# Small value products woven with strips of the neighbouring unit, and layer 0's transposes in half-row tiles: four layers of local attention and gated MLP

## The chip, the cores and the metric

The kernel runs on one NeuronCore of a Trainium2 chip, in one launch. The metric is device time in microseconds (us); lower is better. A profile is taken of one execution with the hardware profiler; its span reaches from the first to the last instruction. TensorE is PE in the profile (its weight loads are PEld), VectorE is DVE, ScalarE is ACT, GpSimd is POOL, SyncE is SP.

## The reference

One sequence of S = 2048 tokens with D = 448 features in bf16 goes through four layers. Layers 0 and 2 are attention with 16 heads of 28 over eight keys, each two positions apart; layers 1 and 3 are a gated product with F = 1792. Both attention layers share weights, and so do both gated ones.

```
def _A_ref(x, wqkv, wo):
    qkv = (x @ wqkv).reshape(B, S, 3, H, Dh).transpose(2, 0, 3, 1, 4)
    q, k, v = qkv[0], qkv[1], qkv[2]
    idx = arange(S)[:, None] - (arange(8) * 2)[None, :]
    logits = einsum("bhsd,bhswd->bhsw", q, k[:, :, idx]) * Dh ** -0.5
    attn = softmax(where(idx >= 0, logits, -1e9))
    o = einsum("bhsw,bhswd->bhsd", attn, v[:, :, idx])
    return o.transpose(0, 2, 1, 3).reshape(B, S, D) @ wo

def _B_ref(x, w_gate, w_up, w_down):
    return ((x @ w_gate) * (x @ w_up)) @ w_down

x = x + _A_ref(layernorm(x), wqkv, wo)
x = x + _B_ref(layernorm(x), w_gate, w_up, w_down)
x = x + _A_ref(layernorm(x), wqkv, wo)
x = x + _B_ref(layernorm(x), w_gate, w_up, w_down)
```

## The kernel before

Everything stays on the chip between layers. Even and odd positions are stored apart, so that the eight keys of a token are neighbours. Tokens are 16 blocks of 128; the chunks that a layer works on are 256 or 512 tokens. A job is one chunk of one layer: `SEQ` names them, A for attention and B for the gated layers ("A00" is layer 0, chunk 0). Jobs of different layers overlap.

A job of an attention layer has these units, in a function each:

- `ln_chunk`: VectorE makes the statistics of each block (`bn`, L630; `mv`, L632), ScalarE the reciprocal deviation (L633, L635), VectorE the normalized block `xn_sb` (L651). It is transposed into `xnTa` or `xnTb`: for layer 0's five chunks (`PE_T`) by TensorE, four 128x128 products a block into one PSUM bank (L660) and a copy by VectorE or ScalarE (L666); for the others by a transposing DMA that SP issues (L654).
- `qk_chunk` and `v_group`: queries, keys and values, from products with 64 rows in two halves of the array (L698, `twin`), copied out of PSUM (L750, L842). The last four heads' values go through DRAM (`PW` copies L759, transposing DMA L770).
- `attn_front`: a score burst, 64 products of 28 rows in tiles of 32x64 (L862), for one group of up to 120 query positions of two blocks; ScalarE's exponential (L869), VectorE's mask (L879).
- `attn_back`: a value burst, 64 products in tiles of 64x32 with 64 columns each (L896; 32 products with 72 columns in a layer's first group), copies into a slot of `O_sb` (L910, L914), and `norm`: a shuffle by VectorE (L924), logarithm and exponential by ScalarE (L925, L926), and VectorE's multiply into `oT` (L937).
- `y_blocks`: output projection (L714, `twin_blocks`) and the addition to `x_sb` (L954).

`b_chunk` is a gated job: for each of 14 slices of F, seven steps of two products with 64 rows, gate in the upper half of the array's rows and up in the lower (L983); ScalarE copies the gate to `g_sb` (L989), VectorE multiplies it with up into `hT` (L992); then products with `WD` for two blocks at a time (L714) and the addition (L954). The last two blocks of the last job end in whole 128x128 tiles, one of 448 columns and two of 224 (L1004, L1008), then output.

A **step** below is what two 64-row products do side by side on the two halves of the array, into two PSUM banks. A **unit** is one `sc.add("pe", ...)` with its steps.

No order is written by hand. Every operation is an `Op` with an estimate, dependencies, a priority (job position plus the tables `PR` and `JP`) and a shape of tiles (`mode`): "R64" (`MAIN`) for 64x128, "R32" for score bursts, "C32" for value bursts, "F" for whole tiles. `Sched.schedule` runs through modelled time and takes for each free engine the ready operation of best priority that finds its PSUM banks; on TensorE it holds units of another shape back (`HOLD_A`, `HOLD_BA`, `HOLD_BB`), since a change of shape has a modelled cost (`SWITCH`). `emit` writes each engine's list in that order, with semaphore waits ahead of each operation. So all estimates and tables shape the order on all five engines, SP's DMAs included.

The head: 48 warm-up products (L565) while inputs load, then the first blocks' transposes.

Of the kernel before, what the change touches and what calls it, by code (L numbers as in the profile page):

```python
# [9 lines left out]
S = 2048  # L10
D = 448
H = 16
DH = 28
F = 1792
# [13 lines left out]
MAIN = "R64"  # L28
PE_T = ("00", "01", "02", "03", "04")
HEAD_LN = 5  # L30
HEAD_P = (-53.71, -30.23, -20.33, -12.94, -19.33)
# [4 lines left out]
S_EST = 270.0  # L36
# [6 lines left out]
VT = 4  # L43
# [8 lines left out]
PR = {'AV': 8.84, 'rstd': -5.66, 'bn': 0.73, 'N': -2.82, 'Gps': -1.08, 'Tps': 16.85, 'H': 18.16, 'S': 10.61, 'VT': 19.61, 'Ex': 16.77, 'G': -2.93, 'xn': -6.19, 'QK': -6.56, 'Ddps': -26.52, 'V': 22.93, 'x': -0.84, 'lnv': -15.5, 'Oc': -6.51, 'Oa': -6.47, 'R': -19.3, 'VVps': 1.22, 'Yps': -25.3, 'PW': 58.69, 'T': -9.57, 'mv': 2.02, 'Rs': -2.57, 'Rl': 21.52, 'QKps': 4.71, 'E': -7.15, 'wqk': -9.31, 'wqp': -11.53}  # L52
JP = {'A20': -3.02, 'B32': 16.28, 'B34': 16.21, 'A22': 20.13, 'B13': 2.73, 'A21': 6.27, 'B12': -2.81, 'A02': -0.21, 'A03': 4.03, 'B30': 4.3, 'B31': 8.23, 'B10': 21.86, 'B11': -14.15, 'A23': 29.86, 'A04': -0.79, 'B33': 153.62, 'A01': -5.33, 'B14': 4.53, 'A00': -24.6}
# [15 lines left out]
A_CAP = 4  # L69
B_CAP = 8  # L70
# [42 lines left out]
class Op:  # L113
    __slots__ = ("engs", "ins", "est", "deps", "mode", "prio", "acquire", "release", "idx", "eng",
                 "dma", "lat", "after", "start", "end", "seen", "selfd", "tmin")
# [14 lines left out]
class Sched:  # L130
# [6 lines left out]
    SWITCH = 92.0  # L137
    FETCH = 4.17
    CREDIT = 36.0
    HICCUP = 210.0  # L140

    def __init__(self):
        self.ops = []
        self.ready = {}
        self.rng = random.Random(SEED)

    def add(self, engs, ins, est, deps=(), prio=0.0, mode=None, acquire=None, release=(), dma=None, lat=0.0, after=None, selfd=(), tmin=None):
        if isinstance(engs, str):
            engs = (engs,)
        if not isinstance(est, dict):  # L150
            est = {e: float(est) for e in engs}
        op = Op(engs=engs, ins=ins, est=est, deps=[d for d in deps if d is not None], mode=mode, prio=prio,
                acquire=acquire, release=release, idx=len(self.ops), dma=dma, lat=lat, after=after, selfd=set(selfd), tmin=tmin)
# [63 lines left out]

    def schedule(self):
# [6 lines left out]
        credit, clast = self.CREDIT, 0.0  # L225
# [6 lines left out]
        for op in self.ops:  # L232
# [9 lines left out]
            if not srcs:  # L242
                for e in op.engs:
                    pend[e].append(op)
        left = len(self.ops)
        now = 0.0
        while left:
            moved = False
            b_ready = any(o.acquire is not None and o.acquire.kind == 1 for o in pend["pe"])
            for e in self.ENGS:  # L250
# [4 lines left out]
                for op in pend[e]:  # L255
                    r = self.ready_at(op, e)
                    if r <= now + 1e-6:
                        cands.append((op.prio, op.idx, op))
# [40 lines left out]
                if best is None:  # L299
                    continue  # L300
                op = best
                op.eng = e
                for x in op.engs:
                    pend[x].remove(op)
                if op.acquire is not None:
                    op.acquire.b = self.pick_banks(op.acquire, now)
                    for b in op.acquire.b:
                        self.holder[b] = op.acquire
                        if self.last_rel[b] is not None:
                            op.deps.append(self.last_rel[b])  # L310
                if op.tmin is not None and e == "sp":
                    gate = [o for o in order["pe"] if o.end + self.PE_LAT <= now and isinstance(o.ins[-1][1], tuple) and o.ins[-1][1] in self.ready]
                    op.deps.append(gate[-1].ins[-1][1])
                est = op.est[e]
                if e == "pe":
                    if mode is not None and op.mode != mode:
                        est += self.SWITCH
                    mode = op.mode
                    n = 2 * len(op.ins)
                    credit = min(self.CREDIT, credit + (now - clast) / self.FETCH)  # L320
                    if n > 40:
                        est = max(est, (n - credit) * self.FETCH + (self.HICCUP if n > credit + 40 else 0.0))
                    credit = max(0.0, credit + est / self.FETCH - n)
                    clast = now + est
                op.start, op.end = now, now + est
                free[e] = op.end
                order[e].append(op)
                for bk, i in op.release:
                    b = bk.b[i]
                    assert self.holder[b] is bk  # L330
                    self.holder[b] = None
                    self.free_at[b] = op.end + self.TAIL[op.eng]
                    key = ("rel", op.idx, b)
                    self.ready[key] = (op, len(op.ins) - 1)
                    self.last_rel[b] = key
                left -= 1
                moved = True
                for u in users.get(op.idx, ()):
                    ndep[u.idx] -= 1
                    if ndep[u.idx] == 0:  # L340
                        for x in u.engs:
                            pend[x].append(u)
# [3 lines left out]
            for e in self.ENGS:  # L346
# [4 lines left out]
                else:  # L351
                    c = [self.ready_at(op, e) for op in pend[e]]
# [9 lines left out]
    def emit(self, nc, block, sems):  # L362
# [10 lines left out]
        for e in self.ENGS:  # L373
            for op in self.order[e]:
# [5 lines left out]
                for n in range(len(op.ins)):  # L380
# [42 lines left out]
def pe_cols(n):  # L423
    return n / 2.4 + 2.6
# [710 lines left out]
```

## Time and profile before

| | |
|---|---|
| runs | 392.64, 393.89, 394.48 us; median 393.89 |
| profiled execution, span | 391.9 us, 2.0 below the median run |
| granted TensorE clock | 1.000 |
| instructions | 13910 |
| products on TensorE | 6142 |
| TensorE idle in gaps, by what ended them | "issue" 0.9, a DMA 0.9, VectorE 0.6 + 0.5, start 1.1 us |
| DMA | 22.47 MB, mean 57 GB/s |

The page gives busy time by engine, the chain of work that ended last (each step followed back to what released it), and the costliest groups of instructions: line, engine, operation, output<-inputs, partitions x elements, count, then busy time, mean of one in ns, and the engine's idle time before them with what ended it. "64\*128" on a product is the tile, rows x columns. "issue" marks idle time in which the profile shows nothing to wait for. A timeline row has start, length, engine, line and count of neighbouring instructions of one kind.

### The profile page before, as it was taken

The page shows a single profiled execution, that of the slowest core. Times are in us where ns is not written, and L with a number is a line of the kernel's source. Part 1 is how long each engine was busy: PE and PEld are TensorE (multiplying, and loading weights), DVE is VectorE, ACT ScalarE, POOL GpSimd, SP SyncE. Part 2 cuts the span into 40 slices and gives each one's busy share as a digit, 9 for nine tenths or more (in the row PEclk, how much of TensorE's full clock was granted, in tenths as well). Part 3 has the DMA queues.
Part 4 walks back from the last instruction along what each step waited for, and adds up shares of the span by engine and source line. Part 5 has one row for each costly group of instructions (what it writes and reads, how often), then busy time and mean ns, then how long its engine had stood idle before and what let it go on. Part 6 is the DMA issues. An engine that isn't in the chain of part 4 may idle for free.

```text
span 391.9 us, 13910 instructions
## 1 busy us (share of the span) xinstructions
PE 384.9 (98%) x6142; PEld 213.8 (55%) x6142; DVE 271.2 (69%) x596; ACT 207.3 (53%) x398; POOL 7.6 (2%) x36
## 2 busy tenths in 40 slices
PE   8999999999999999999999999999999999999997
PEld 6655657545444544554546867444454544444674
DVE  6989899669967765684788645258942689477252
ACT  4888876478523745467651523268315782263230
POOL 6010000000000000000000000000000000000000
DMA  8990161501220401320121141010050102403101
GB/s 275 295 306 19 24 93 28 106 13 30 48 49 15 80 15 35 64 28 15 17 49 21 36 95 29 25 20 11 12 128 7 26 7 47 95 4 16 34 27 47
DMA packets 54703, 22.47 MB, mean 57 GB/s; under 512 B 44836, under 2 KB 54644, under 8 KB 54644
## 3 DMA queue, kind: packets, MB, share of 16 engines
q1 hardware_dynamic: 53284, 19.47, 23.7%
q10 hardware_dynamic: 1360, 2.12, 1.8%
q8 instruction: 48, 0.79, 0.8%
q14 instruction: 11, 0.09, 0.1%
HBM read 8.54 MB, written 2.71 MB: 29 GB/s over the span
## 4 chain that ended last, share of the span: by engine, by line
PE 90%; DVE 4%; DMA 2%; ACT 2%; issue 1%; SPq 0%; DVEq 0%
PE ps L983 41%; PE ps L714 25%; PE ps L698 16%; PE ps L896 3%; PE ps L862 3%; PE ps L1004 1%; DMA xnTb<-xn_sb 1%; DMA x_sb<-in_A_x_dram 1%; PE ps L660 1%; DVE xn_sb L651 1%; DVE st L630 1%; DVE x_sb L954 1%; ACT R_sb L925 1%; ACT R_sb L926 1%; DVE E_sb L879 0%
## 5 line engine op out<-in xcount | busy, mean ns | idle before, releaser
L983 PE MATMUL ps<-xnTb,WGU 64*128 64x512 bf16 (+1 forms) x1960 | 180.5, 333 | 0.9 <-DMA xnTb<-xn_sb 0.9
L983 PEld LDWEIGHTS ps<-xnTb,WGU 64*128 64x128 bf16 x1960 | 93.5, 94 | 73.8 <-ACT g_sb L989 1.5
L989 ACT ACTIVATE g_sb<-ps 128x512 bf16<-128x512 f32 (+1 forms) x140 | 71.4, 511 | 95.0 <-PE ps L983 94.3
L992 DVE TENSOR_TENSOR hT<-g_sb,ps 128x512 bf16<-128x512 bf16 (+1 forms) x140 | 79.3, 574 | 55.1 <-ACT g_sb L989 46.1
L714 PE MATMUL ps<-WD,hT 64*128 64x448 bf16 x840 | 84.0, 349 | 0.1
L714 PEld LDWEIGHTS ps<-WD,hT 64*128 64x128 bf16 x840 | 40.2, 94 | 37.0 <-DVE hT L992 0.8
L698 PE MATMUL ps<-xnTa,WQK 64*128 64x512 bf16 (+1 forms) x504 | 53.5, 353 | 0.3
L954 DVE TENSOR_TENSOR x_sb<-x_sb,ps 128x448 bf16<-128x448 bf16 x62 | 36.2, 614 | 24.9 <-PE ps L714 24.8
L630 DVE BATCH_NORM_STATS2 st<-x_sb 128x6 f32<-128x448 bf16 x64 | 37.5, 615 | 2.7 <-DMA x_sb<-in_A_x_dram 2.7
L869 ACT ACTIVATE E_sb<-ps 128x1024 bf16<-128x1024 f32 (+1 forms) x36 | 33.5, 980 | 9.6 <-PE ps L862 9.3
L750 ACT ACTIVATE qk<-ps 128x1024 bf16<-128x1024 f32 (+1 forms) x30 | 27.1, 921 | 19.3 <-PE ps L698 19.0
L651 DVE TENSOR_SCALAR xn_sb<-x_sb,mv,rstd 128x512 bf16<-128x512 bf16 (+1 forms) x64 | 33.7, 569 | 4.7 <-ACT rstd L635 4.5
L698 PEld LDWEIGHTS ps<-xnTa,WQK 64*128 64x128 bf16 x504 | 23.5, 94 | 24.0 <-ACT xnTa L666 0.8
L879 DVE TENSOR_TENSOR E_sb<-E_sb,MK 128x1024 bf16<-128x1024 bf16 (+2 forms) x40 | 23.9, 613 | 8.8 <-ACT E_sb L869 8.5
L714 PE MATMUL ps<-wo_g,oT 64*128 64x448 bf16 x256 | 29.1, 349 | 0.0
L633 ACT ACTIVATE lnv<-mv,eps_sb 128x2 f32<-128x2 f32 (+1 forms) x33 | 9.5, 293 | 30.4 <-DVE mv L632 30.2
L937 DVE TENSOR_TENSOR oT<-O_sb,R_sb 128x480 bf16<-128x480 f32 (+3 forms) x36 | 22.1, 627 | 3.4 <-ACT R_sb L926 3.1
L925 ACT ACTIVATE R_sb<-R_sb 128x480 f32<-128x480 f32 (+1 forms) x34 | 20.1, 600 | 5.6 <-DVE R_sb L924 5.6
L924 DVE STREAM_SHUFFLE R_sb<-O_sb 128x480 f32<-128x480 f32 (+1 forms) x34 | 22.7, 696 | 0.0
L698 PE MATMUL ps<-WV,xnTa 64*128 64x336 bf16 (+3 forms) x252 | 22.2, 304 | 0.2
L926 ACT ACTIVATE R_sb<-R_sb 128x480 f32<-128x480 f32 (+1 forms) x34 | 20.1, 602 | 0.4
L714 PEld LDWEIGHTS ps<-wo_g,oT 64*128 64x128 bf16 x256 | 12.3, 94 | 11.6 <-DVE oT L937 0.4
(47 smaller groups left out, 170.7 us busy)
## 6 DMA issues: line engine op xcount, KB each, us to landing
out_dram<-x_sb SPq DMA_DIRECT2D x15, 112.0 KB, 1.7
WD<-in_B_w_down_dram SPq DMA_DIRECT2D x2, 784.0 KB, 11.5
WGU<-in_B_w_up_dram SPq DMA_DIRECT2D x2, 784.0 KB, 17.6
WGU<-in_B_w_gate_dram ACTq DMA_DIRECT2D x2, 784.0 KB, 13.3
x_sb<-in_A_x_dram SPq DMA_DIRECT2D x3, 448.0 KB, 6.4
vt<-qk SPq DMA_DIRECT2D x42, 16.0 KB
xnTb<-xn_sb SPq DMA_TRANSPOSE x32, 3.0
x_sb<-in_A_x_dram SPq DMA_DIRECT2D x2, 224.0 KB, 4.2
```

The source lines that it names most:

```text
L630: sc.add("dve", one(lambda E, B=B: E.bn_stats(st6[:, B, :], x_sb[:, B, :]), ("bn", li, B)), 525.0, deps=[("x", li - 1, B)] + ([("xn", li - ...
L651: sc.add("dve", one(lambda E, B=B, dst=dst, src=src: E.tensor_scalar(dst, src, mv[:, B, 0:1], rstd[:, B:B + 1], ALU.subtract, ALU.mult), ( ...
L698: parts[0 if s < 3 else 1][1].append((lambda E, w=w, c=c, lo=lo, st=st, sp_=sp_: E.matmul(u["out"](w), u["lhs"](w, c, lo, lo + 64), u["rhs ...
L714: ins.append((lambda E, w=w, c=c, lo=lo, st=st, sp_=sp_: E.matmul(outs(w), lhs(w, c, lo), rhs(w, c, lo), start=st, stop=sp_), keys[w] if s ...
L750: return E.activation(dst, src, ACT.Copy) if hasattr(E, "activation") else E.tensor_copy(dst, src)
L869: return E.activation(E_sb[:, slot, 2 * hp:2 * hp + 2, 0:w], ps[:, b0:b0 + 2, 0:w], ACT.Exp, scale=SCALE)
L925: sc.add("act", one(lambda E: E.activation(R_sb[:, rs, 0:w], R_sb[:, rs, 0:w], ACT.Ln), ("Rl", li, qb)), act_est(w, False), deps=[("Rs", l ...
L926: sc.add("act", one(lambda E: E.activation(R_sb[:, rs, 0:w], R_sb[:, rs, 0:w], ACT.Exp, scale=-1.0), ("R", li, qb)), act_est(w, False), de ...
L954: sc.add("dve", one(lambda E: E.tensor_tensor(x_sb[:, B, :], x_sb[:, B, :], ps[:, bk[w], 0:D], ALU.add), ("x", li, B)), dve_est(D), deps=[ ...
L983: ins.append((lambda E, u=u, k=k, w=w: E.matmul(u["out"](w), WGU[64 * w:64 * w + 64, k, 128 * u["fc"]:128 * u["fc"] + 128], X[64 * w:64 * ...
L989: sc.add("act", one(lambda E, gs=gs, bk=bk: E.activation(g_sb[:, gs, 0:nt], ps[:, bk[0], 0:nt], ACT.Copy), ("G", li, j, fc)), act_est(nt), ...
L992: sc.add("dve", one(lambda E, gs=gs, bk=bk, fc=fc: E.tensor_tensor(hT[:, fc, hs, 0:nt], g_sb[:, gs, 0:nt], ps[:, bk[1], 0:nt], ALU.mult), ...
```

## The change

*Strips.* `crossed`, `twin`, `twin_blocks` and `b_chunk` now hand over their units as steps, and `pair` makes two forms of each: the two products as before, and eight strips of 64x32, four for each half, with the same moving data and columns. When the scheduler places a value burst (`BURST`), it looks for a ready unit in 64x128 tiles, takes it as host, and lays its first steps as strips into the burst: two steps for 64 products (`WEAVE`, `MAXALT`), after 21 and 42 of them, one for 32. The host's remaining steps follow at once in whole products. All waits of burst and host stand ahead of the burst.

*Transposes and warm-up.* A block of layer 0 is transposed by eight products of 64 rows and 64 columns into two banks in place of four of 128x128 into one; the copy reads both banks. The 48 warm-up products become 96 of 64 rows. Their shape is `MAIN`.

*Value bursts* wait for the last reader of the `O_sb` slots that their copies write, which the copies alone waited for.

*The model and its tables.* TensorE's time in the scheduler now has a queue and instruction lines (`run_pe`), other estimates (`S_EST`, `AV_EST`, `SWITCH`), other caps on banks, a limit on how far gate units run ahead (`after`), and `PR`, `JP` and `HEAD_P` are all new. The order on every engine is new.

```diff
+BURST = "C32"
+WEAVE = 2
+MAXALT = 2
...
-S_EST = 270.0
+S_EST = 288.0
+AV_EST = 288.0
...
-A_CAP = 4
-B_CAP = 8
+A_CAP = 6
+B_CAP = 6
...
+                    if op.mode == BURST and WEAVE:
+                        host = next((m for m in okay if m is not op and m.mode == MAIN and len(m.alt) and (m.acquire is None or self.pick_banks(m.acquire, now) is not None)
...
+                        if host is not None:
+                            take(host)
+                            got.append(host)
+                            k = min(len(host.alt), WEAVE * len(op.ins) // 64)
...
+                            cut = [len(op.ins) * (i + 1) // (k + 1) for i in range(k)] + [len(op.ins)]
+                            seq, a = [], 0
+                            for i, z in enumerate(cut):
+                                seq += [(op, n) for n in range(a, z)]
+                                a = z
+                                if i < k:
+                                    seq += [(host, fn) for fn in host.alt[i]]
+                            seq += [(host, n) for n in range(2 * k, len(host.ins))]
...
+def pair(calls):
+    def whole(out, lhs, rhs, start, stop):
+        return lambda E: E.matmul(out(), lhs(), rhs(), start=start, stop=stop)
+    def strip(out, lhs, rhs, start, stop, row, c):
+        return lambda E: E.matmul(out()[c:c + 32], lhs()[:, c:c + 32], rhs(), start=start, stop=stop, tile_position=(row, c))
+    ins = [(whole(*a[:5]), a[6]) for a in calls]
+    strips = [strip(*a[:6], c) for a in calls for c in range(0, 128, 32)] if all(a[6] is None for a in calls) else None
+    return ins, strips
+def alt_of(strips, keep=1):
+    n = 0
+    while n < len(strips) - keep and strips[n] is not None:
+        n += 1
+    return strips[:min(n, MAXALT)]
...
-        sc.add("pe", one(lambda E: E.matmul(ps[:, wb[0], 0:256], warm[:, 0:128], warm, start=True, stop=True), ("warm", n)), 214.0 if n < WARM else 109.0, deps=["c_warm"], mode="F",
+        ins = [(lambda E, h=h: E.matmul(ps[:, wb[h], 0:256], warm[64 * h:64 * h + 64, 0:128], warm[64 * h:64 * h + 64], start=True, stop=True), ("warm", n) if h else None) for h in range(2)]
+        sc.add("pe", ins, 214.0 if n < WARM else 109.0, deps=["c_warm"], mode=MAIN,
...
-                    ins.append((lambda E, c=c, slot=slot, bk=bk: E.transpose(ps[:, bk[0], :].bitcast(bf)[:, 128 * c:128 * (c + 1)], xn_sb[:, slot, 128 * c:128 * (c + 1)], ident[:]),
-                                ("Tps", li, B) if c == 3 else None))
-                sc.add("pe", ins, 4 * 56.0, deps=[("xn", li, B), "c_id"], mode="F", acquire=bk, prio=prio)
+                    for h in range(2):
+                        ins.append((lambda E, c=c, h=h, slot=slot, bk=bk: E.transpose(ps[:, bk[h], :].bitcast(bf)[:, 64 * c:64 * c + 64], xn_sb[64 * h:64 * h + 64, slot, 128 * c:128 * (c + 1)],
+                                                                                      ident[64 * h:64 * h + 64, 64 * h:64 * h + 64]), ("Tps", li, B) if (c, h) == (3, 1) else None))
+                sc.add("pe", ins, 4 * 29.3, deps=[("xn", li, B), "c_id"], mode=MAIN, acquire=bk, prio=prio)
...
-        sc.add("pe", ins, S_EST * nd / 2, deps=[("E", li, g, 0), ("E", li, g, 1), "c_v"] + [(k, li, q) for k in ("V", "VT") for q in qbs], mode="C32", acquire=bk, prio=prio)
+        sc.add("pe", ins, AV_EST * nd / 2, deps=[("E", li, g, 0), ("E", li, g, 1), "c_v"] + [(k, li, q) for k in ("V", "VT") for q in qbs] + [r[1] for r in oring], mode=BURST, acquire=bk, prio=prio)
...
-            sc.add("pe", ins, 7 * pe_cols(nt), deps=u["deps"] + tdeps, mode=MAIN, prio=prio, acquire=u["bk"])
+            sc.add("pe", [i for st, _ in steps for i in st], 7 * pe_cols(nt), deps=u["deps"] + tdeps, mode=MAIN, prio=prio, acquire=u["bk"], alt=alt_of([st for _, st in steps]),
+                   after=gu_ops[-NG] if len(gu_ops) >= NG else None)
```

## The prediction

> **What bounds the kernel now.** I read the page's first part and its chain, then TensorE's groups by shape, its timeline around a few bursts, busy time by stage, and last the end of the run.
>
> ```profile
> PE 384.9 (98%) x6142; PEld 213.8 (55%) x6142; DVE 271.2 (69%) x596; ACT 207.3 (53%) x398; POOL 7.6 (2%) x36
> ...
> PE 90%; DVE 4%; DMA 2%; ACT 2%; issue 1%; SPq 0%; DVEq 0%
> ```
>
> TensorE has work nearly all the time and 90% of the chain that ended last is its own. So an edit is worth what it takes out of TensorE's stream, unless something else is then late. Its groups by shape:
>
> ```profile
> L983 PE MATMUL ps<-xnTb,WGU 64*128 64x512 bf16 x1176 | 134.8, 376 | 0.9 <-DMA xnTb<-xn_sb 0.9
> L714 PE MATMUL ps<-WD,hT 64*128 64x448 bf16 x840 | 84.0, 349 | 0.1
> ...
> L896 PE MATMUL ps<-E_sb,v_sb 64*32 64x64 bf16 x1024 | 11.5, 195 | 1.0 <-issue 0.9
> L862 PE MATMUL ps<-qk 28*64 28x64 bf16 x1024 | 11.3, 202 | 0.6 <-DVE WQK L581 0.6
> ...
> L660 PE MATMUL ps<-ident,xn_sb 128*128 128x128 bf16 x64 | 5.0, 220 | 0.5 <-DVE xn_sb L651 0.5
> ```
>
> Durations overlap, so I price by intervals from start to start. Two 64-row products run side by side: such a pair takes 215.8 ns at 512 columns, 189.2 at 448, 109.2 at 256. What concerns us are the value bursts (L896), 64 small products in 64x32 tiles, and the transposes (L660) in whole 128x128 tiles:
>
> ```profile
> 82.45 0.68 PE L896 MATMUL ps<-E_sb,v_sb 64*32 64x64 bf16 x64
> 83.06 1.69 PE L983 MATMUL ps<-xnTb,WGU 64*128 64x512 bf16 x14
> 84.68 0.71 PE L862 MATMUL ps<-qk 28*64 28x64 bf16 x64
> 85.32 1.50 PE L714 MATMUL ps<-WD,hT 64*128 64x448 bf16 x14
> 86.78 0.54 PE L896 MATMUL ps<-E_sb,v_sb 64*32 64x64 bf16 x47
> 88.09 0.26 PE L896 MATMUL ps<-E_sb,v_sb 64*32 64x64 bf16 x17 [0.78 <-issue]
> ```
>
> An undisturbed value burst takes 0.615 us (82.45 to 83.065). Its single starts in the trace show why: the first 31 products go eight in 29 ns, all eight tiles at work; then a hole of 107 ns; then one per 8.3 ns to the end. The burst at 86.78 stops for 0.78 us with nothing waited for, and afterwards its last 17 products go at the fast pace again. I read this as instructions coming too slowly: 62 (a product and its weight load each) are at hand, and from 235 ns after the start one comes every 4.17 ns. Changing tile shape costs too: the last pair before a burst takes 93 ns longer (306 against 213).
>
> ```profile
> 9.41:50.00 40.59, 39.72 (x859) 23.14 (x860) 37.23 (x95) 34.06 (x67) 1.64 (x6) 1.00 0.60 163
> 50.00:95.00 45.00, 43.10 (x918) 25.91 (x916) 37.70 (x90) 30.88 (x62) 0.00 (x0) 1.00 0.31 53
> 95.00:390.00 295.00, 294.32 (x4316) 158.81 (x4312) 190.59 (x397) 137.84 (x261) 0.00 (x0) 1.00 0.19 37
> ```
>
> After the first pair of numbers (length, TensorE) come weight loads, VectorE and ScalarE. Until 95 us VectorE is nearly as full as TensorE (37.2 of 40.6 us, then 37.7 of 45); later it has a third free. A gain in the first stage can end in a wait for VectorE.
>
> **The change, part by part.** The changed order on TensorE contains what the diff says: in all 16 full value bursts two pair steps stand as eight strips each, in one half burst one step; 33 steps: 13 of 512 columns, 14 of 448, 6 of 256, together 13 x 215.8 + 14 x 189.2 + 6 x 109.2 = 6.1 us of pair time.
>
> 1. *Strips in bursts.* A strip has a small product's tile but a whole step's columns. Eight small products run side by side in 29 ns, so I take eight strips as one step of unchanged length. Now: 0.615 + 2 steps. With all instructions in time: 15 + 63 x 3.65 + 130 (last start to the next unit) = 0.375 us + 2 steps, 0.24 less; for 16 bursts 3.8. With the supply read above (62 at hand, 4.17 ns each from 235 ns on; the burst now needs 160), the second strips are issued at 402 to 460 ns instead of 390 to 420, and a burst with 512 columns lasts 0.86 instead of 1.05, with 448 0.81 instead of 0.99, with 256 0.77 instead of 0.83: 13 x 0.185 + 3 x 0.06 = **-2.6**. I take this, as it follows the 8.3 ns row; bounds -3.8 and 0. The 16 bursts now take 11.70, so 1.9 go to stops (0.9 at 86.78, the rest mostly in the four double bursts). The changed order has no doubles, but score bursts within 1 us behind a value burst at three places, so I return **-1.2** (bounds 0 and -1.9). Four more entries: **+0.4**.
>
> A rule speaks against strips: the Trainium skill, "TensorEngine Tiling (Array Packing)", Restrictions and Gotchas, says that column tiling excludes Fast Weight Load, and "TensorE: Matmul & The Clock Gate", LDWEIGHTS, gives a load's time as columns / 1.2 ns; eight loads of 32 columns one after another would be 213 ns, and if these did not hide, the 33 steps would cost their time again and the sum would be an estimated 394.8. The measured 29 ns for eight such loads and products decides against it.
>
> Another does too: "Runtime: NRT & Kernel Launch", Instruction fetch mechanics, calls instruction fetch hidden by the pace of issue; then the 8.3 ns would be TensorE's own, bursts would save nothing, and the sum would be 391.3. The 0.78 us marked "issue", and the pace after it, speak for supply.
>
> 2. *Transposes and warm-up.* After 9.41 us there are 56 transposes, in the trace 4.42 us with the switch behind each group and 0.59 before them; 0.66 of it is a wait (counted in 3): 4.35. They become 112 with 64 columns, 56 pairs. No row shows this; 29 ns for 64 columns is the nearest: 1.64; **-2.7**. If two do not run side by side, 59 ns a pair and -1.1. That the shape is the neighbours' removes the switches. The 48 warm-up products become 48 pairs of the same length: 0.
>
> 3. *New order: VectorE.* I added up each engine's new order with the intervals that the same operations have in the trace when they follow without a gap, and compared at each wait of TensorE: TensorE's products alone bring it to a score unit at 22.4 us, VectorE's queue to the copies it needs at 23.3; 32.0 against 32.9; 45.5 against 45.8; 85.3 against 85.1. In the order of before, VectorE's sum leads by 0.6 to 3 us everywhere. VectorE falls behind its bare sum: now 1.4 us at 26.5, 2.9 at 31, 4.2 at 48, 5.4 at 73, of which 2.4 are small holes and 3.0 waits. So TensorE will stand between 3.2 (holes and a third of the waits: 2.4 + 1.0 - 0.2) and 5.2 us (5.4 - 0.2) behind its bare sum at 87 us. Now it stands 5.3 behind there, with the 0.9 stop that 1 has counted: 4.4. I take **0**; bounds -2 and +4. The value burst's new wait, for the last reader of its output slots, lies here: behind it is all of TensorE; the second burst comes to it at 35.7, the multiply is through VectorE's sum at 36.4, which is no worse than the points above. On SP, seven value transposes now stand ahead of the second pair of layer 1's second chunk; the last value transposes wait for a burst at 64.8: 64.8 + 4.5 + 4 issues of 1.35 + 3.0 to landing = 77.7, the products come at 76.7 + 4.5 = 81.2: hidden, 3.5 to spare. After 95 us VectorE's lead grows, and the chunks come 13 us or more behind the blocks they are made from.
>
> 4. *The end.* Now:
>
> ```profile
> 379.60 0.42 DVE L992 TENSOR_TENSOR hT<-g_sb,ps 128x256 bf16<-128x256 bf16 x1 [0.34 <-ACT g_sb L989]
> 379.75 1.49 PE L714 MATMUL ps<-WD,hT 64*128 64x448 bf16 x14
> 379.95 0.38 ACT L989 ACTIVATE g_sb<-ps 128x256 bf16<-128x256 f32 x1 [0.38 <-PE ps L983]
> 380.36 0.42 DVE L992 TENSOR_TENSOR hT<-g_sb,ps 128x256 bf16<-128x256 bf16 x1 [0.34 <-ACT g_sb L989]
> 381.17 2.82 PE L1004 MATMUL ps<-WD,hT 128*128 128x448 bf16 x14
> ```
>
> After the last gate and up products TensorE has 14 others, while ScalarE and VectorE make the last part of hT. In the new order the closing products follow directly; they need that part, ready at 380.78 when the products ended at 379.75: +1.0, less two changes of shape, **+0.8** (bounds 0 and 1.2).
>
> 5. *The head.* One more pair of small activations (0.19 + 0.09) stands on ScalarE before the transposed copy that releases the first unit; that copy waits 0.16 now: **+0.15** (0 to 0.4).
>
> Sum: -2.6 - 1.2 + 0.4 - 2.7 + 0 + 0.8 + 0.15 = -5.15. Span 391.9 to 386.75. The median run is 393.89, 2.0 above the profiled span: **388.7 us**.
>
> **Rivals.**
> - *More is had* (15%): supply does not bind (-1.2 more) and VectorE's holes alone remain (-2): **385.5**. For it: ScalarE has 6 us less in its queue (174 against 181). Against: VectorE has 9 more (264 against 256).
> - *VectorE takes it back* (17%): its lag by 87 us is 12.7 now, once waits that cost nothing are in. If the new queue lags halfway between 5.2 and this, 3.75 more: **392.5**, no change. For it: no spare at four points. Against: most of those waits are for TensorE itself.
> - *Instructions run out* (12%): 310 more products pass; if woven bursts stop as the one at 86.78 did, each costs 0.89. From the ninth it is slower by over 0.5%; at ten 388.7 + 8.9 - 0.7 (left in the sum) = **396.9**. For it: 160 instructions a burst instead of 128. Against: strips hold the queue for two steps, 11 bursts of 16 have 2.8 us or more of long products on both sides, and of the eight single ones now only one has stopped so long.
> - *It does not do what it says*: excluded, the strips are in the order; that they might run one row group at a time is against the 29 ns, and is under the 12%.
>
> **How the numbers follow.** Forecast 56%. A measurement of this kernel tells about 0.5% from no change: 391.9 to 395.9 is "same". Faster: 56 + 15 + 4 of the third case = 75%; same 13%; slower 12%. The range leaves out the fourth case and the best of the second, takes in the third and most bounds: 385.0 to 393.5.
>
> **What would show it.** Right: value bursts with strips of 0.8 to 0.9 us; pairs of transposes at 29 ns without the 93 ns; waits of TensorE for VectorE summing to some 4 us before 95 us; 1.0 us of idle before the last product group; no "issue" stops beyond one. Wrong: strips longer than a step, "issue" above 2 us, or waits before 95 us of 8 and more.

## The result, and the profile after

The changed kernel takes **396.51 us** (median of 11 runs, 394.08 to 397.70) against 393.58 (11 runs, 392.55 to 394.48): a ratio of 1.0066, 95% interval 1.0046 to 1.0085. It is slower by 2.9 us where 5.15 less were forecast, so 8.1 us are to be found. The profiled execution took 396.39 us, with a span of 394.6. In 10 of the 11 runs the granted clock is 0.995 or 0.996; in all of the kernel before it is 1.000.

The page of the changed kernel:

```profile
PE 382.7 (97%) x6452; PEld 215.6 (55%) x6452; DVE 279.5 (71%) x604; ACT 200.8 (51%) x390; POOL 8.0 (2%) x36
...
PEclk9998999999999999999999999999999999999999
...
q8 instruction: 51, 0.84, 0.9%
...
PE 88%; DVE 4%; ACT 2%; DMA 2%; issue 2%; SPq 1%; DVEq 0%
...
L511 PE MATMUL ps<-xnTa,WQK 64*128 64x512 bf16 (+1 forms) x500 | 54.4, 361 | 4.5 <-issue 3.3
```

TensorE is busy for 2.2 us less than before, as it should be, yet the span is 2.7 longer. Two things are new: 3.3 us of idle time ahead of layer 0's query and key products with nothing that they waited for ("issue"), and a slice of the clock line below 9, the fourth. Both lie early, as the busy time by stage shows (columns as in the prediction):

```profile
9.41:50.00 40.59, 34.39 (x774) 20.28 (x774) 32.90 (x82) 27.00 (x56) 0.73 (x4) 0.96 0.52 156
50.00:95.00 45.00, 44.78 (x1180) 29.51 (x1180) 43.00 (x102) 35.92 (x70) 0.00 (x0) 1.00 0.40 55
95.00:390.00 295.00, 293.83 (x4373) 158.19 (x4370) 196.86 (x403) 133.22 (x255) 0.00 (x0) 1.00 0.20 37
```

In the first stage TensorE is busy for 34.4 of 40.6 us, 5.3 less than before. In the second it is fuller than before (44.8 against 43.1). I added up TensorE's products at their undisturbed pace (the **bare sum**; small products in woven bursts at 3.7 ns, so each of these bursts counts some 0.15 us as lost) and took the difference to their start in the trace: the changed kernel is 1.6 us behind its bare sum at 20 us, 8.4 at 36, 10.0 at 50 and 11.9 at 95 (before: 0.3, 1.7, 1.9, 5.4; its bare sum is 6.3 us longer). So the loss is made between 14 and 36 us. TensorE's timeline there:

```profile
21.46 0.82 PE L511 MATMUL ps<-xnTa,WQK 64*128 64x512 bf16 x6
23.27 1.04 PE L511 MATMUL ps<-xnTa,WQK 64*128 64x512 bf16 x8 [0.99 <-issue]
...
26.49 0.82 PE L511 MATMUL ps<-xnTa,WQK 64*128 64x512 bf16 x6 [0.82 <-DVE WQK L683]
...
27.89 0.72 PE L511 MATMUL ps<-xnTa,WQK 64*128 64x256 bf16 x8
30.92 5.34 PE L511 MATMUL ps<-xnTa,WQK 64*128 64x512 bf16 x56 [2.32 <-issue]
```

Both stops without a wait fall into a row of equal products. From start to start, less the undisturbed interval, they cost 1.2 and 2.5 us. The single starts show the rest: from 32.1 to 35.5 us, 3.413 us long, the granted clock is 0.5 and pairs of 256 columns take 213 ns instead of 109: 1.6 us. The other new waits are smaller: 1.2 us at 15 us (a score burst for VectorE's copy of `qk`), the 0.82 shown.

The parts that the prediction priced are there. A woven burst, in the timeline:

```profile
36.19 0.27 PE L1004 MATMUL ps<-E_sb,v_sb 64*32 64x64 bf16 x21
36.28 0.40 PE L514 MATMUL ps<-xnTa,WQK 64*32 64x512 bf16 x8
36.50 0.25 PE L1004 MATMUL ps<-E_sb,v_sb 64*32 64x64 bf16 x21
36.58 0.53 PE L514 MATMUL ps<-xnTa,WQK 64*32 64x512 bf16 x8
36.81 0.39 PE L1004 MATMUL ps<-E_sb,v_sb 64*32 64x64 bf16 x22
37.13 0.39 PE L511 MATMUL ps<-xnTa,WQK 64*128 64x512 bf16 x2
```

From 36.19 to 37.13 are 0.94 us for burst and two steps; each eight strips take one step's time, 0.22. The transposes run in pairs, one pair per 29 ns, with no change of shape. And at the end TensorE waits 0.93 us for the last part of `hT`:

```profile
386.69 5.50 PE L1110 MATMUL ps<-WD,hT 128*128 128x448 bf16 x42 [0.93 <-DVE hT L1098]
```

### The profile page after: what moved, and what is told of

Its sections match the earlier page's. It is cut to its first block, busy times and chain, and to the rows that moved or that the text cites. A ratio compares the mean times of both kernels' runs of the same rounds, so it can differ in the third digit from the quotient of the medians.

```text
span 394.6 us, 14517 instructions
## 1 busy us (share of the span) xinstructions
PE 382.7 (97%) x6452; PEld 215.6 (55%) x6452; DVE 279.5 (71%) x604; ACT 200.8 (51%) x390; POOL 8.0 (2%) x36
## 4 chain that ended last, share of the span: by engine, by line
PE 88%; DVE 4%; ACT 2%; DMA 2%; issue 2%; SPq 1%; DVEq 0%
PE ps L511 80%; PE ps L967 3%; PE ps L1004 2%; DMA x_sb<-in_A_x_dram 2%; PE ps L514 2%; PE ps L1110 1%; SPq L601 1%; ACT E_sb L974 1%; DVE R_sb L1029 1%; ACT R_sb L1030 1%; DVE st L732 1%; DVE O_sb L1015 0%; DVE oT L1042 0%; DVE hT L1098 0%; DVE xn_sb L753 0%
## 5 line engine op out<-in xcount | busy, mean ns | idle before, releaser
L511 PE MATMUL ps<-xnTb,WGU 64*128 64x512 bf16 (+1 forms) x1926 | 174.5, 333 | 0.2
L511 PE MATMUL ps<-WD,hT 64*128 64x448 bf16 x828 | 81.1, 349 | 0.0
L511 PE MATMUL ps<-xnTa,WQK 64*128 64x512 bf16 (+1 forms) x500 | 54.4, 361 | 4.5 <-issue 3.3
L974 ACT ACTIVATE E_sb<-ps 128x1024 bf16<-128x1024 f32 (+1 forms) x36 | 33.9, 979 | 8.2 <-PE ps L967 7.9
L855 ACT ACTIVATE qk<-ps 128x1024 bf16<-128x1024 f32 (+1 forms) x20 | 18.8, 939 | 18.0 <-PE ps L511 17.8
L511 PE MATMUL ps<-wo_g,oT 64*128 64x448 bf16 x240 | 27.6, 350 | 0.2
L855 DVE CAST qk<-ps 128x1024 bf16<-128x1024 f32 (+1 forms) x16 | 17.4, 1088 | 13.0 <-PE ps L511 13.0
L735 ACT ACTIVATE lnv<-mv,eps_sb 128x2 f32<-128x2 f32 (+1 forms) x33 | 9.5, 294 | 32.1 <-DVE mv L734 31.7
L511 PE MATMUL ps<-WV,xnTa 64*128 64x336 bf16 (+3 forms) x252 | 23.1, 304 | 0.5 <-ACT xnTa L769 0.5
```

What stands on the lines that cost most here:

```text
L511: return lambda E: E.matmul(out(), lhs(), rhs(), start=start, stop=stop)
L855: return E.activation(dst, src, ACT.Copy) if hasattr(E, "activation") else E.tensor_copy(dst, src)
L974: return E.activation(E_sb[:, slot, 2 * hp:2 * hp + 2, 0:w], ps[:, b0:b0 + 2, 0:w], ACT.Exp, scale=SCALE)
```

## What stops TensorE

The row `q8 instruction` of the page gives the lead: 51 DMA packets on the instruction queue, each of 16 KB in the trace. TensorE's part of the trace has 13034 instructions (a product and its weight load each, and the waits), which is 51 blocks of 256. In program order the two stops stand behind instructions 704 and 960, each 64 ahead of a multiple of 256. I call such a place a **boundary**. The long stop of the kernel before, in the burst at 86.78 us, stands at one too (3520). Times from the trace's DMA packets:

| kernel, boundary | boundary before passed | packet | TensorE goes on |
|---|---|---|---|
| changed, instruction 704 | 448 at 14.4 us | 20.68 to 21.74 | 23.27, after a stop |
| changed, 960 | 704 at 23.3 | 28.55 to 29.54 | 30.92, after a stop |
| before, 704 | 448 at 19.4 | 23.05 to 24.24 | 25.4, no stop |
| before, 3520 | 3264 at 84.4 | 85.64 to 86.70 | 88.09, after a stop |

TensorE resumes 1.4 to 1.5 us after a packet ends, and where the weights load (370 GB/s at 20 to 25 us) a packet starts 5.3 and 6.2 us after the boundary before was passed. The traces of all kernels here, with those of the experiments, have 38 stops of TensorE of over 0.25 us that the profile marks "issue": every one stands at a boundary, and ends 1.2 to 1.6 us after a packet of the instruction queue. Theory **Supply**: blocks of 256 instructions come late, because the warm-up (96 more) and the transposes (128 more over layer 0) bring TensorE to the boundaries earlier, while the weights fill the DMA engines; the half clock follows from the idle time. Rivals: **Order** (the new tables make TensorE wait, whatever the count) and **Strips** (woven bursts cost more than they give).

## The experiments

**1. Whole warm-up products** in the changed kernel, 96 instructions fewer (`a_warm_whole`):

```diff
-ins = [(lambda E, h=h: E.matmul(ps[:, wb[h], 0:256], warm[64*h:64*h+64, 0:128], ...), ...) for h in range(2)]
+ins = [(lambda E, h=h: E.matmul(ps[:, wb[0], 0:256], warm[:, 0:128], warm, ...) if h else None, ...) for h in range(2)]
```

> The changed kernel, its order on every engine kept; only the 48 warm-up pairs are one whole 128x128 product each again, of the same length: 48 products, or 96 instructions (a product and its weight load), fewer on TensorE before 15 us. Theory Supply (the loss is the two stops without a wait at 21.9 and 28.2 us, 3.7 us, and the 3.4 us of half clock after them, 1.6 us; they come because TensorE reaches the 256-instruction blocks that its instruction queue must bring earlier than before, while the weights fill the DMA engines): the block boundaries come about 2 us of work later, the stops shrink from 3.7 to under 1.5 us and the half clock goes: 392.0 to 394.5 us against 396.5. Theory Order (the new order makes TensorE wait for VectorE early, whatever the instruction count): 396.0 to 397.0.

394.76 us (12 runs; 393.10 to 396.51; ratio to before 1.0036, 1.0017 to 1.0055): 1.75 less than the changed kernel. But it is not as Supply had it: the stops did not shrink, they moved to other work, to the same instruction numbers (704, 960, now 1216 too; 1.2, 1.4 and 1.7 us). What went is the half clock: 8 of 12 runs are at clock 1.000 (median 394.6, the other four 396.2).

**2. Doubled warm-up** in the kernel before (`b_warm_double`): each warm-up product of 256 columns as two of 128.

```diff
-one(lambda E: E.matmul(ps[:, wb[0], 0:256], warm[:, 0:128], warm, ...), ...)
+[(lambda E, h=h: E.matmul(ps[:, wb[0], 128*h:128*h+128], warm[:, 0:128], warm[:, 128*h:128*h+128], ...), ...) for h in range(2)]
```

> The kernel before, its order kept; only each of the 48 warm-up products of 256 columns is cut into two of 128 columns, of the same length together: 96 instructions more on TensorE before 15 us, the same count as the changed kernel's warm-up. Supply: stops without a wait appear between 20 and 32 us, 1 to 4 us together: 394.5 to 398 against 393.6. Order, or strips as the cause: 393.3 to 394.0.

397.78 us (8 runs, 394.18 to 400.02; ratio 1.0098, 1.0064 to 1.0132). 96 instructions that take no time cost 4.1 us. The profiled execution is one of the two without half clock (394.42); it has the stop at instruction 960, here in a score burst, and one of 1.1 us at instruction 2240 (56 us):

```profile
28.22 0.51 PE L862 MATMUL ps<-qk 28*64 28x64 bf16 x41
30.75 0.29 PE L862 MATMUL ps<-qk 28*64 28x64 bf16 x23 [2.02 <-issue]
```

The other six, at clock 0.996, have a median of 398.2. Order and Strips explain none of it: this kernel has the old order and no strips.

**3. No strips** in the changed kernel's order (`a_no_strips`): the burst alone, the two steps whole behind it.

```diff
-for i, z in enumerate(cut):
-    seq += [(op, n) for n in range(a, z)]
...
+seq = [(op, n) for n in range(len(op.ins))] + [(host, n) for n in range(len(host.ins))]
```

> The changed kernel, its order kept; only the strips are undone: each of the 16 full value bursts runs by itself, and the two product steps that stood in it follow whole. 462 instructions fewer over the whole run. By step 1 of the prediction, strips save 0.185 us at each 512- or 448-column burst and 0.06 at each 256-column one: 2.6 us slower than the changed kernel, 399.1. Theory Strips (the woven bursts cost more than they give, by entries and instructions): 394 to 396. Supply and Order both say that what is lost early has little to do with strips: the two stops at 21.9 and 28.2 us stay, as no woven burst comes before 36 us.

397.46 us (6 runs, 396.34 to 398.59): 0.95 slower, in place of 2.6, and Strips is out. (It has 396 instructions fewer in the trace, not 462.) The two stops are there (4.4 us of "issue"). Beside the changed kernel product by product, every full burst costs 0.09 to 0.12 more, and at a few places much of this comes back: the changed kernel loses 0.24 among the `WD` products at 76 us, 0.21 in the score burst at 79.36 (0.85 us against 0.64), and 0.11, 0.11, 0.13 and 0.26 ahead of products at 222.6, 224.4, 240.0 and 267.6 us. The first two are late blocks again: they stand at boundaries 3264 and 3520, and end 1.5 and 1.4 us after a packet (74.95 to 76.45, 78.60 to 79.98). What the other four wait for is open.

**4. Whole transposes** in the changed kernel (`a_trans_whole`): four 128x128 products a block, one bank.

```diff
-E.transpose(ps[:, bk[h], :].bitcast(bf)[:, 64*c:64*c+64], xn_sb[64*h:64*h+64, slot, 128*c:128*(c+1)], ident[64*h:64*h+64, 64*h:64*h+64])
+E.transpose(ps[:, bk[0], :].bitcast(bf)[:, 128*c:128*(c+1)], xn_sb[:, slot, 128*c:128*(c+1)], ident[:]) if h else None
```

> The changed kernel, its order kept; only layer 0's transposes are whole 128x128 tiles again: 64 products of 128 columns for 128 of 64, so 128 instructions fewer over layer 0, but a change of shape before and behind each group. By step 2 of the prediction: 2.7 us slower than the changed kernel where TensorE sets the time, 399.2. Supply: the stops shrink as in the run with whole warm-up products, as some 100 of the 128 instructions come before 36 us, and this takes back 2 to 4 us of the 2.7: 395 to 397.5. Order: 398.5 to 399.5.

399.40 us (4 runs, 398.71 to 400.17): 2.9 slower, as step 2 and Order have it, and outside Supply's range. But the profiled execution has 5.5 us of "issue" (the changed kernel: 3.3), now at boundaries 960, 1216, 2752 and 3264, and 6.8 us of half clock, so it measures more than transposes. Experiments 13 and 17 separate that.

**5 to 7. Weights in pieces**: SyncE's loads of layer 1's up and down weights as 28 pieces of 112 KB, each behind a wait for TensorE's progress (`a_paced`; `a_paced_warm` with whole warm-up products too; `b_paced` on the kernel before).

```diff
-E.dma_start(dst, src)
+E.wait_ge(sems["pe"], min(v for (oi, _), v in value.items() if self.ops[oi].eng == "pe" and self.ops[oi].end >= 17000 + 1000 * j))
+E.dma_start(dst[:, k], src[:, k])
```

> The changed kernel, its order on TensorE, VectorE, ScalarE and GpSimd kept; only SyncE's four loads of layer 1's up and down weights (3.2 MB, which land by 27 us) are cut into 28 pieces of 112 KB, issued one by one as TensorE gets on, about one per us from 17 to 45 us. They are first needed at 60 us. Instruction count as in the changed kernel. Theory Supply in its sharper form (a 256-instruction block takes 3.8 us from being asked for to being usable in quiet stretches, and 7 to 9 us while the weights fill the DMA engines): the stops at 21.9 and 28.2 us go from 3.7 to under 0.5 us, the half clock goes, shorter stops may remain where 256 instructions pass in under 4 us: 391.0 to 393.5. If the blocks are late whatever else is loaded: 395.5 to 396.5. Order: 396 to 397.

> Both edits on the changed kernel: weights in paced pieces, and the 48 warm-up pairs as whole products (96 instructions fewer). Supply: with the blocks in time the count matters little: within 0.7 us of the run with paced weights alone, 390.5 to 393. If the count decides by itself, 1.5 us or more below the paced run alone. Order: 396.

> The kernel before with its weights in the same paced pieces, orders kept. Its profile shows no stop without a wait before 50 us, so Supply expects nothing: 393.2 to 394.0. If pacing by itself helps (less load for the other transfers, say), 392 or less, and the paced changed kernel must be compared with that.

400.78, 400.58 and 402.14 us (5, 4 and 4 runs): all misses, the control most of all. The pieces kept SyncE's queue busy until 51 us, so that what it issues behind them was late: 3.6 us of waiting for `xnTb` in the first, 3.0 for the values and 2.9 behind them in the third, each with half clock after it. And the gate weights, on ScalarE's queue, still filled the DMA engines at 16 to 24 us; the stop at 704 stayed. Only the quiet stretch behind it told something: the next block's packet came 1.1 us after its boundary, not 5.3, and there was no stop at 960.

**8. The old tables** in the changed kernel (`a_old_tables`).

```diff
-HEAD_P, PR, JP, A_CAP, B_CAP = (those of the changed kernel)
+HEAD_P, PR, JP, A_CAP, B_CAP = (those of the kernel before)
```

> The changed kernel with the planner's tables of the kernel before (the priorities by operation and by job, the head's, and the two limits on blocks in hand); strips, transposes and warm-up stay as changed, the planner makes a new order of them. Order (the new tables make the loss): 389 to 393. Supply: early stops come with this order too, as the instruction count before 36 us is the same: 395 to 398, with 2 to 5 us of stops without a wait before 50 us.

414.06 us (6 runs, 411.57 to 415.27), outside both ranges. So it is not the new tables that lose: with strips and half-row transposes, the old tables are 17.5 us worse, with a single stop of 5.8 us without a wait (at boundary 960) and 20 us of half clock.

**9 to 12. All of layer 1's weights late.** From here on the 75 transposes by DMA are plain copies of the same size, so that rows arrive untransposed and later values are wrong; `p_after` and `p_before` are the two kernels with that edit only. `p_late` takes gate, up and down weights out of the crowded stretch; `p_late_warm` has whole warm-up products as well.

```diff
-E.dma_start_transpose(X[:, :, c0:c0+128], xn_sb[:, slot, 0:128*nt])
+E.dma_start(X[:, :, c0:c0+128], xn_sb[:, slot, 0:128*nt].rearrange("p (c n) -> p c n", n=128))
-E.dma_start_transpose(v2_sb[:, slot, :], vt_dram[li][:, k0:k0+128])
+E.dma_start(v2_sb[:, slot, :], ones32[:])
```

> Control for the next ones. The changed kernel, every engine's order kept; only the 75 transposes by DMA are plain copies of the same size (layer 1 to 3's normalized rows arrive untransposed, and the values of the pairs come from a tile of ones), so what is computed is wrong from layer 1 on, and the load is much the same. The first of these copies starts at 54 us, so the run up to there is the changed kernel's own. All theories: the stops at instructions 704 and 960 (21.9 and 28.2 us) and the half clock as in the changed kernel, in total within 2 us of its 396.5.

> The control with all of layer 1's gate, up and down weights late: gate and up alternating from SyncE in 28 pieces of 112 KB, one per 0.7 us from about 18 us, the down weights in 14 pieces after 40 us behind the first stores of values. (The paced run before had left the gate weights on ScalarE's queue; these alone kept the DMA engines full, share 1.06 at 20 to 24 us, so it tested little before 24 us. Behind that, with a share under 0.5, a block asked for at 24.4 us started after 1.1 us, against 5.3 us in the changed kernel, and the stop at instruction 960 was gone.) Supply: the stops at 704 and 960 (3.7 us) go and the half clock with them: 3 to 5.5 us below the control. If a block is late without such load as well, or the order makes the loss: within 1 us of the control.

> As the run with late weights, and the 48 warm-up pairs as whole 128x128 products (96 instructions fewer). Supply: with the blocks in time the count matters little: within 0.7 us of that run. If the count decides by itself: 1.5 us or more below it.

> The kernel before with the same plain copies for its 75 transposes by DMA: what is computed is wrong from layer 1 on. It gives the difference that the rest of the change makes where late weights have taken the stops away: by the prediction's sum, without stops, the run with late weights should be 4 to 5 us below this one; this one itself within 2 us of the kernel before.

| kernel | us (runs) | behind its bare sum at 50 us |
|---|---|---|
| `p_after` | 396.31 (12), as the changed kernel | 11.1 |
| `p_late` | 398.21 (4) | 4.2 |
| `p_late_warm` | 400.65 (6) | 5.5 |
| `p_before` | 391.73 (7), 1.7 below the kernel before | |

In `p_late` both stops and the half clock are gone up to 50 us. Busy time of `p_late`:

```profile
20.00:25.00 5.00, 4.10 (x96) 2.09 (x92) 4.91 (x18) 4.50 (x10) 0.82 (x4) 1.00 0.58 161
25.00:30.00 5.00, 4.93 (x132) 3.53 (x128) 4.50 (x11) 4.51 (x11) 0.00 (x0) 1.00 0.49 139
30.00:35.00 5.00, 4.96 (x198) 3.17 (x192) 4.67 (x11) 3.71 (x6) 0.00 (x0) 1.00 0.59 165
```

and of the changed kernel:

```profile
20.00:25.00 5.00, 3.96 (x92) 1.83 (x90) 3.89 (x11) 3.33 (x8) 0.00 (x0) 1.00 1.06 370
25.00:30.00 5.00, 2.79 (x98) 1.55 (x94) 4.40 (x14) 5.00 (x10) 0.73 (x4) 1.00 0.69 207
30.00:35.00 5.00, 4.02 (x42) 2.53 (x44) 2.37 (x5) 1.56 (x4) 0.00 (x0) 0.71 0.01 3
```

Read the first column after the stretch (TensorE) with the last two (DMA share, GB/s): where the DMA share was 1.06 with 370 GB/s, TensorE stood next; at 0.5 to 0.6 it is full from 25 us on. From 21 us on, packets start 0.6 to 1.1 us after the boundary before instead of 5 to 6. VectorE's 4.5 to 4.9 of 5 us, against 2.4 to 4.4, fit that it, too, had stood for TensorE. The total was a miss again, for a new wait: the down weights' 14 pieces held SyncE's queue until 52.7 us, TensorE waited 6.1 us for `xnTb` at 54 us, and 6.8 us of half clock followed. `p_late_warm` shows that load is not the whole: with 96 instructions fewer, a boundary (1216) falls into a score burst right behind a value burst, 2.1 us behind the boundary before, and it stops for 1.6 us with the DMA engines half empty (share 0.64 and 0.47 around it).

**13 to 15. Fewer, larger pieces**, out of SyncE's queue by 37.6 us (`p_late2`), the control (`p_before_late2`), and without strips (`p_late2_no_strips`).

```diff
-for k in range(7)
+for k in ((0, 2), (2, 4), (4, 6), (6, 7))   # k[0]:k[1]; down weights ((0, 4), (4, 7))
```

> The changed kernel with plain copies for its transposes by DMA (values wrong from layer 1 on), and layer 1's weights late in 20 larger pieces (gate and up 16 of 224 or 112 KB, alternating, one per us from about 17 us, then the down weights in four), all out of SyncE's queue by 37 us. Supply alone is the cause: no stop at 704 and 960, no half clock, no wait of 6 us for the normalized rows: 398.2 - 6.1 - 3.4 = 388.7, range 388 to 391, that is 5 to 8 us below its control (396.3) and 1 to 4 below the kernel before with the same copies (391.7). Another cost in the order behind 50 us, or the half clock comes without the stops: 393 or more.

> The kernel before with the same copies and the same late weights: control. It has no stop without a wait before 50 us, so late weights give nothing there: 391.0 to 392.5 (its control: 391.7). If late weights help by themselves, by less load for other transfers: 390 or less.

> As p_late2, with the strips undone (each value burst by itself, the two steps whole behind it). By step 1 as measured (a burst with two 512-column steps 0.945 us against 1.046, 0.1 each): 16 bursts, 1.6 us slower than p_late2 where TensorE sets the time; by step 1 as predicted: 2.6; if a wait for VectorE or a late block takes the gain back as it did in the changed kernel: under 0.8.

**390.53 us** (6 runs, 390.18 to 391.83, clock 1.000 in all): 5.8 below `p_after`, and the first version below both kernels with the same copies: 1.2 below `p_before`, 1.4 below `p_before_late2` (391.93, 9 runs), to which late weights give nothing, as expected. It keeps the changed kernel's order, so Order is out as well. Without strips it takes 390.86 (6 runs, 390.74 to 391.56): the strips are worth 0.3, no more than the runs of one kernel differ. The profiled execution of `p_late2`, the slowest of its six, has stops of 0.3 and 0.7 us at boundaries 1472 and 3520, that of the kernel without strips 0.2 in all: more instructions bring late blocks here too.

**16 and 17. Whole transposes, and the boundaries moved back** (`p_late2_trans`; `p_late2_trans_pad` cuts 32 warm-up pairs into two column halves, 128 instructions that take no time).

```diff
+for c in ((0, 128), (128, 256)) if n < 32 else ((0, 256),):
-    E.matmul(ps[:, wb[h], 0:256], warm[64*h:64*h+64, 0:128], warm[64*h:64*h+64], ...)
+    E.matmul(ps[:, wb[h], c[0]:c[1]], warm[64*h:64*h+64, 0:128], warm[64*h:64*h+64, c[0]:c[1]], ...)
```

> As p_late2 (plain copies for the transposes by DMA, values wrong from layer 1 on; layer 1's weights late), with layer 0's transposes as whole 128x128 tiles again, 64 products for 128, and a change of shape before and behind each group. By step 2 as predicted, where TensorE sets the time: 2.7 us slower than p_late2's 390.5, 393.2. If TensorE waits for VectorE at the same places anyway (VectorE as the bound up to 45 us), the transposes give little: 390.5 to 391.5, and step 2 had priced work that lies beside a wait.

> As p_late2_trans (398.8 us), with 32 of the 48 warm-up pairs cut into two column halves each: 64 products, or 128 instructions, more on TensorE before its first real product, for the same warm-up time. Behind layer 0's transposes every instruction then has the number that it has in p_late2, whose blocks came in time. Supply: 128 instructions more make it faster by 4 to 6 us; without stops what is left against p_late2 is step 2's price, 2.7 us as predicted: 393.2. If the number of instructions, and not where the boundaries fall, makes the stops: 398.8 or more.

398.79 us (6 runs, 396.96 to 401.40), and with the 128 instructions put back **392.52** (12 runs, 392.14 to 393.14, clock 1.000 in all). More instructions made it 6.3 us faster. The same score burst in the two, first without them:

```profile
33.35 0.39 PE L530 MATMUL ps<-xnTa,WQK 64*128 64x512 bf16 x2
33.67 0.48 PE L985 MATMUL ps<-qk 28*64 28x64 bf16 x37
36.81 0.42 PE L985 MATMUL ps<-qk 28*64 28x64 bf16 x27 [2.66 <-issue]
```

and with them:

```profile
33.20 0.39 PE L530 MATMUL ps<-xnTa,WQK 64*128 64x512 bf16 x2
33.52 0.71 PE L989 MATMUL ps<-qk 28*64 28x64 bf16 x64
34.15 1.04 PE L530 MATMUL ps<-xnTa,WQK 64*128 64x512 bf16 x8
```

Without them, boundary 960 stands at 31.8 us and 1216 in this burst at 33.9, with a woven burst between: 256 instructions in 2.2 us. The packet for the block came at 34.02 to 35.33. Two more stops, of 1.7 and 1.1 us, stand at boundaries 2752 and 3264, and 3.413 us of half clock begin at the end of the first. With them, the boundaries before and behind stand at 27.8 and 32.8, and the burst does not stop; one stop of 0.5 us is left (boundary 1472). This settles Supply: not how many instructions there are, but how fast TensorE passes from one boundary to the next, against how long a block takes to come. The 2.0 us between 392.52 and 390.53 are the price of whole transposes, with the same blocks in time. They come from two sessions, and the kernel before, measured beside them, took 393.80 and 393.18: against it the price is 1.4.

## Why the prediction was wrong

| step | predicted | measured |
|---|---|---|
| 1 strips and entries | -2.6 + 0.4 | -0.3 (13 against 15), late blocks included |
| 1 stops returned | -1.2 | not isolated |
| 2 transposes | -2.7 | -2.0 (13 against 17); -1.4 with each taken against the kernel before beside it |
| 3 order, VectorE | 0 | not isolated |
| 4 end | +0.8 | +0.8: 1.1 of wait, less 0.3 for three changes of shape |
| 5 head | +0.15 | +0.26 |
| late blocks, half clock | no term | +5.8 (9 against 13); +5.5 taken likewise |

The measured terms sum to +4.6, or +4.9 with the second figures. With plain copies the change costs 396.31 - 391.73 = 4.6, so they nearly close there. With the real transposes it costs 2.9; the kernel before alone loses 1.7 from them. Its profiled execution has 0.9 us of stops and waits 0.9 for `xnTb`; that of `p_before` has 0.2 of stops and no such wait, which makes 1.6 of the 1.7. The stops are part of the 1.2 that step 1 returned; that the change itself returns them is argued, not shown.

- **The step that failed** is the one that has no line: the prediction priced no stop outside the bursts. It saw a stop without a wait, read it as "instructions coming too slowly", and made of it a supply of single instructions to a burst. The 4.17 ns pace may be that; the 0.78 us stop is not. It was a late block (boundary 3520, packet ended at 86.70, TensorE went on at 88.09), and what sets such a stop is how fast TensorE passes the 256 instructions between two boundaries, and how long the next block takes to come. Late blocks and the half clock behind them cost 5.8 us; its own sign of being wrong, "issue" above 2 us, came (3.3). So "the 48 warm-up products become 48 pairs of the same length: 0" was right in time and wrong in price: in the kernel before, 96 such instructions cost 4.1 us.
- **The rival "Instructions run out"** had the right resource, at 12%, and a time (396.9) that is close, by the wrong mechanism: it put the stops into woven bursts, one each. Neither of the two stops before 36 us is in one, so that the time is close is luck.
- **Step 1**: the mechanism was right, the size was not. Woven bursts take 0.94, 0.885 and 0.75 us (512, 448 and 256 columns) against 0.86, 0.81 and 0.77; without strips 1.046, 0.993 and 0.833. The last 22 small products start every 9.4, 8.4 and 5.3 ns on average, not every 3.7. I read this as too few instructions at hand after two steps, which no run shows by itself. 16 bursts give 1.6, and most of that is lost again, at late blocks and other later waits (experiments 3 and 15).
- **Step 2**: right in mechanism, 1.4 to 2.0 against 2.7.
- **Step 3**: the bounds were -2 to +4. In `p_late2` TensorE is 7.5 us behind its bare sum at 90 us; less 1.0 of stops without a wait and 0.15 at each of seven woven bursts, which step 1 has, this leaves 5.4 against the 4.4 forecast, in an execution that took 1.3 us longer than the median. So VectorE as the bound fits; its term is not isolated.
- **Steps 4 and 5** were right. At the end the wait is 1.1 us from the last gate products to the closing ones, less 0.31 at 381.17, 383.92 and 386.68 us in the kernel before, where its tile shape changed.
- The half clock had no term either. The Trainium skill, "TensorE: Matmul & The Clock Gate", Part 1, gives the activity window as 3413 ns, and the stretches here are 3.413 us or multiples of it. It lets half clock follow an idle window; here it followed with no stop longer than 2.5 us, after 4.6 us of stops and waits between 21.9 and 30.9. What share of idle time sets it off, these runs do not settle.
- The prediction had weighed "Runtime: NRT & Kernel Launch", Instruction fetch mechanics, against the trace, and took from it only the rule that fetch is hidden. The same section says that instructions come in blocks of 256, the next while the current one runs. The trace agrees with that (51 packets of 16 KB) and decides against the rule: at 256 instructions in 2.1 us a block was late even with half of the DMA engines' time free (`p_late_warm`).

What stays open: why the runs of the changed kernel differ (394.1 to 397.7 us). The two stops differ between executions, 1.2 and 2.5 us here and 1.7 and 3.0 in `p_after`, which does the same up to there; that this makes the spread is not shown. Open, too, is why plain copies spare the kernel before the stop at 86.78.

## What to carry to other kernels

Count instructions, not only time: on an engine that runs hundreds of small products, find where each block of 256 ends, and what it passes in the next 4 us. Spread large loads, or start them after the first blocks, but see what they block in the queue that issues them. A stop with nothing waited for is worth its own line in the sum, with the question which packet ended 1.4 us before it ended.

## What was not expected of the hardware

In quiet stretches, a block of 256 instructions that TensorE stands for starts to load some 1 us after the boundary before is passed, takes 0.9 to 1.5 us, and TensorE goes on some 1.4 us after: mostly 3.0 to 4.1 us in all. In the changed kernel it was 7.6 and 8.8 while weights load at 320 to 370 GB/s. Stops of 1.2 to 2.5 us within 9 us were enough for 3.413 us of half clock, which costs 1.6 us of TensorE's time; in experiment 2 the runs with it are 3.9 us longer than those without, so they must hold longer waits as well, which no trace here shows. 128 instructions that did nothing made a kernel 6.3 us faster.
